# A state-space scan and a memory attention in one kernel: V projection moved beside the scan, Q/K projection interleaved with a key-by-query attention

## The chip, the cores and the metric

One core of one Trainium2 chip. The time is device microseconds of that core, the median of several executions; lower is better. Engine names: PE is the matmul engine and PEld its weight loads, DVE the vector engine, ACT the scalar engine, POOL the GpSimd engine, SP the engine that here only issues DMA. "L336" in a profile line is line 336 of the kernel that was profiled.

## The reference, cut to what matters

The output is two unrelated results side by side: part A is a complex diagonal state-space scan over 2048 steps with 1024 states; part B is an attention over 64 segments of 32 tokens, each of which also sees 8 memory rows, where the memory of a segment is the output of the segment before it.

```python
def _A_ref(x, Lambda_re, Lambda_im, B_re, B_im, C_re, C_im, log_dt, Dskip):   # x: 1 x 2048 x 1024
    # ... Lam_bar, B_bar from the parameters ...
    Bu = jnp.einsum('bld,pd->blp', x + 0j, B_bar)
    for t in range(L):
        h = Lam_bar[None, :] * h + Bu[:, t, :]
        hs.append(h)
    y = 2.0 * jnp.einsum('blp,dp->bld', hseq, Cmat).real + x * Dskip[None, None, :]

def _B_ref(x, mem0, Wq, Wk, Wv, Wo, seg_len):      # 32 heads of 128, M = 8, seg_len = 32
    for s in range(n_seg):
        xs = x[:, s * seg_len:(s + 1) * seg_len, :].copy()
        h = jnp.concatenate([mem, xs], axis=1)
        q = jnp.einsum('btd,dhe->bhte', h, Wq)     # k and v likewise
        scores = jnp.einsum('bhqe,bhke->bhqk', q, k) * scale
        scores = jnp.where(mask[None, None], scores, -1000000000.0)
        p = _softmax(scores, axis=-1)
        o = jnp.einsum('bhqk,bhke->bhqe', p, v)
        o = jnp.einsum('bhte,hed->btd', o, Wo)
        mem = o[:, :M, :].copy()
        outs.append(o[:, M:, :])
return jnp.concatenate([a, b], axis=-1)
```

Both kernels avoid the 64 sequential steps in the same way. They guess every segment's memory from the mean of its rows, compute all segments at once with the guess, compare the memory that comes out with the guess, and repeat in a slower way only if the two differ by more than a tolerance (2^-8).

One caution for all that follows. With these inputs the attention half of the reference has a standard deviation of 2.0e-5 and the scan half of 2.5e-3 (computed from the reference). A comparison over the whole output therefore hardly sees an error in the attention half.

## The kernel before

It runs four stages one after the other: part A (scan and its output matmuls); K, V and mean projections of all tokens; Q projection with the guess and the projections of the guessed memory; attention with the output projection. K, V and Q go to DRAM and come back. A unit is 4 segments and 16 heads: scores have queries on partitions, so the probabilities must be transposed by DVE before the product with V, and the memory rows of V are gathered from DRAM in 16 small pieces per unit.

```python
        def load(u):
            g, hh = units[u]; h0 = hh * HH
            d = {}
            e1 = nc.sync
            e2 = nc.scalar
            d["kT"] = ld.tile([128, HH, J, L], BF16, name="s2_kT")
            e2.dma_start(d["kT"][:], scr["kTa"][g, :, h0:h0 + HH, :, :])
# ... cut ...
            d["v"] = ld.tile([128, HH * E], BF16, name="s2_v")
            e2.dma_start(d["v"][:], scr["v"][g * 128:(g + 1) * 128, h0 * E:(h0 + HH) * E])
            vx = vmx[u % NBUF]
            for j in range(J):
                for b in range(4):
                    r0 = (g * J + j) * M
                    src = scr["vm"][r0:r0 + M, h0 * E:(h0 + HH) * E].rearrange("k (a b e) -> k a b e", b=4, e=E)[:, :, b, :]
                    dst = vx[32 * j + 8 * b:32 * j + 8 * b + 8, :, :].rearrange("k (a b) e -> k a b e", b=4)[:, :, b, :]
                    (nc.sync if (j * 4 + b) % 2 == 0 else nc.scalar).dma_start(dst, src)
            d["vx"] = vx
            S.activation(d["kT"][:, :, :, 0:M], km_u[:], ACT.Copy)
```

Softmax in `front`, and the transposes (`PTx`, `PTm`), then the products in `back`:

```python
            mx = sm_.tile([128, nh], FP32, name=f"s2_mx{tag}")
            V.tensor_reduce(mx[:], Sx[:], AX.X, ALU.max)
            Gp.tensor_tensor(Sx[:], Sx[:], mx[:].unsqueeze(2).to_broadcast([128, nh, L]), ALU.subtract)
            S.activation(Sx[:], Sx[:], ACT.Exp)
            sm = sm_.tile([128, nh], FP32, name=f"s2_sum{tag}")
            V.tensor_reduce(sm[:], Sx[:], AX.X, ALU.add)
            V.reciprocal(sm[:], sm[:])
            Px = sm_.tile([128, nh, SEG], BF16, name=f"s2_Px{tag}")
            Pm = sm_.tile([128, nh, M], BF16, name=f"s2_Pm{tag}")
            Gp.tensor_tensor(Px[:], Sx[:, :, M:L], sm[:].unsqueeze(2).to_broadcast([128, nh, SEG]), ALU.mult)
            Gp.tensor_tensor(Pm[:], Sx[:, :, 0:M], sm[:].unsqueeze(2).to_broadcast([128, nh, M]), ALU.mult)
            return Px, Pm
# ... cut ...
                Px, Pm = softmax(pl, HH, cst["maskx"], "x")
                ptx = PTx[u % 2]; ptm = PTm[u % 2]
                for j in range(J):
                    q = slice(32 * j, 32 * j + 32)
                    V.transpose(ptx[q, j, :, :].rearrange("p h k -> p (h k)"), Px[q, :, :].rearrange("p h k -> p (h k)"))
                    V.transpose(ptm[q, j, :, :].rearrange("p a k -> p (a k)"), Pm[q, :, :].rearrange("p h m -> p (h m)"))
# ... cut ...
        def back(u):
            g, hh = units[u]; h0 = hh * HH
            d = st[u]; v_u = d["v"]; vx = d["vx"]
            if do_x:
                ptx = PTx[u % 2]; ptm = PTm[u % 2]
                oT = op_.tile([128, HH, 128], BF16, name="s2_oT")
                for a in range(HH // 4):
                    pO = psO.tile([128, 4, 128], FP32, name="s2_pO")
                    for b in range(4):
                        h = 4 * a + b
                        PE.matmul(pO[:, b, :], v_u[:, h * E:(h + 1) * E], ptx[:, :, h, :], start=True, stop=False)
                        PE.matmul(pO[:, b, :], vx[:, h, :], ptm[:, :, a, :], start=False, stop=True)
                    S.activation(oT[:, 4 * a:4 * a + 4, :], pO[:], ACT.Copy)
```

## Time and profile before

| | before |
|---|---|
| time, median of 3 runs | 1677.34 us (1676.97 to 1678.32) |
| span of the profiled run, mean granted PE clock | 1670.9 us, 0.950 |
| PE busy, idle | 1458.8 us, 212.1 us |
| DMA | 233.72 MB in 224776 packets |

The first part of the profile page: busy time of each engine, its share of the span, and how many instructions.

```profile
span 1670.9 us, 33806 instructions
PE 1458.8 (87%) x14297; PEld 764.0 (46%) x14297; DVE 828.3 (50%) x1869; ACT 425.4 (25%) x793; POOL 148.9 (9%) x240
```

The windows view cuts the span into stretches; the columns are the stretch, its length, the busy time and the number of instructions of each engine, the granted PE clock (1.00 is full), the DMA share and GB/s.

```profile
core 0: us, PE busy (x) PEld busy (x) DVE busy (x) ACT busy (x) POOL busy (x), PEclk, DMA share, GB/s
0.00:348.00 348.00, 287.70 (x1673) 144.68 (x1674) 320.27 (x670) 129.65 (x228) 20.45 (x39) 0.94 0.22 67
348.00:860.00 512.00, 510.53 (x3246) 240.40 (x3246) 103.97 (x165) 84.84 (x145) 8.48 (x4) 1.00 0.45 151
860.00:1160.00 300.00, 252.89 (x2067) 134.36 (x2066) 89.79 (x177) 60.00 (x110) 3.36 (x7) 0.94 0.68 203
1160.00:1671.00 511.00, 407.72 (x7312) 244.58 (x7311) 314.24 (x857) 150.93 (x310) 116.57 (x191) 0.92 0.46 141
```

Length minus PE busy is the time in which PE stands still: 60 us in part A, where DVE is the busy one, 1.5 us in the projections, 47 us in the third stage, and 103 us in the attention. In the attention stage the clock is 0.92 as well, so the matmuls themselves take longer.

The waits view (what an engine waited for; total us, how often, longest) names for the attention stage, on PE and on ACT:

```profile
ACT s_kT L516 <- DMA s_vmx_10121<-b_vm_s: 64.8, 13, 7.3
ACT s_kT L516 <- DMA s_vmx_10122<-b_vm_s: 54.1, 15, 11.2
PE s_pO L586 <- DVE s_PTx_10123 L567: 36.4, 13, 5.1
PE s_pO L586 <- DVE s_PTx_10124 L567: 28.8, 11, 3.1
```

Read alone, the lines of PE say that the DVE transposes cost 65 us, and the lines of ACT that the memory gathers (`s_vmx`) make only ACT wait, which is 30% busy here.

### The profile page before, as it was taken

Reading aid. Unit: us, or ns where it says so; the run is one execution under the profiler, and the core shown is the slowest. Engines: PE = TensorE matmul, PEld = TensorE weight load, DVE = VectorE, ACT = ScalarE, POOL = GpSimd, SP = SyncE. Lnnn points to the kernel's source line nnn. Section 1 sums busy time; section 2 is a strip of 40 time slices with the busy share of each in tenths; the row PEclk is TensorE's granted clock in tenths of the full one; section 3 lists DMA queues with packets and bytes.
Section 4 is the critical chain, followed back from the end, with each engine's and each line's share of the span. In section 5 each row is a group of like instructions: output and inputs, shape, how many; then the busy total and the mean of one; then the engine's idle time right before and its main releaser. Section 6 shows DMA issues by size and latency. Waiting matters only on the chain.

```text
span 1670.9 us, 33806 instructions
## 1 busy us (share of the span) xinstructions
PE 1458.8 (87%) x14297; PEld 764.0 (46%) x14297; DVE 828.3 (50%) x1869; ACT 425.4 (25%) x793; POOL 148.9 (9%) x240
## 2 busy tenths in 40 slices
PE   4789989889999999999999888992888777887787
PEld 2444434444444444444445444441545444454454
DVE  8999999631221121121223322223656666566564
ACT  7742322111111111111121122221223232323322
POOL 1100000020000000000000000001222222222220
PEclk9899999899999999999999999996899999999999
DMA  3430000296415424432363689865444545545432
GB/s 114 128 97 15 28 16 20 82 309 218 138 53 190 139 76 166 139 115 102 121 207 108 195 257 273 252 177 186 130 146 145 157 136 162 159 136 163 136 109 96
DMA packets 224776, 233.72 MB, mean 140 GB/s; under 512 B 61536, under 2 KB 197472, under 8 KB 224616
## 3 DMA queue, kind: packets, MB, share of 16 engines
q1 hardware_dynamic: 154272, 129.08, 25.3%
q10 hardware_dynamic: 68024, 95.04, 17.4%
q0 software_dynamic: 2320, 7.35, 1.3%
q8 instruction: 114, 1.87, 0.5%
q14 instruction: 46, 0.38, 0.1%
HBM read 150.99 MB, written 80.45 MB: 139 GB/s over the span
## 4 chain that ended last, share of the span: by engine, by line
PE 57%; DVE 25%; DMA 8%; POOL 4%; ACT 3%; issue 2%; SPq 1%; ACTq 0%; POOLq 0%; DVEq 0%
PE p_p L320 13%; PE p_p L336 13%; PE p_p L723 11%; DVE a_wr L178 2%; DVE a_wi L179 2%; DVE s_PTx_10123 L567 2%; PE s_pO L587 2%; PE s_pO L586 2%; POOL s_Sxx L534 2%; DVE s_PTx_10124 L567 1%; DMA p_wm<-in_B_Wk_dram 1%; POOL s_Pxx L541 1%; DVE s_Sxx L530 1%; DVE s_mxx L533 1%; DVE s_sumx L537 1%
## 5 line engine op out<-in xcount | busy, mean ns | idle before, releaser
L336 PE MATMUL p_p<-p_w,g_shared 128*128 128x512 bf16 x1024 | 224.6, 379 | 0.0
L723 PE MATMUL p_p<-g_shared,p_w 128*128 128x512 bf16 x896 | 198.9, 381 | 0.3 <-DVE p_stq L261 0.2
L320 PE MATMUL p_p<-g_shared,p_w 128*128 128x512 bf16 x896 | 194.5, 379 | 0.0
L612 PEld LDWEIGHTS <-s_oT 128*128 128x128 bf16 x1024 | 100.1, 103 | 128.8 <-issue 28.9
L336 PEld LDWEIGHTS <-g_shared 128*128 128x128 bf16 x1024 | 98.4, 98 | 118.4 <-issue 2.6
L261 DVE CAST p_stk<-p_p 128x512 bf16<-128x512 f32 x64 | 44.3, 692 | 191.7 <-PE p_p L320 185.8
L723 PEld LDWEIGHTS <-p_w 128*128 128x128 bf16 x896 | 87.2, 98 | 106.4 <-issue 5.4
L320 PEld LDWEIGHTS <-p_w 128*128 128x128 bf16 x896 | 87.1, 98 | 104.1
L261 DVE CAST p_st<-p_p 128x512 bf16<-128x512 f32 x64 | 44.3, 692 | 180.7 <-PE p_p L336 180.7
L261 DVE CAST p_stq<-p_p 128x512 bf16<-128x512 f32 x64 | 44.2, 691 | 168.0 <-PE p_p L723 167.2
L259 ACT ACTIVATE p_st<-p_p 128x512 bf16<-128x512 f32 x64 | 38.2, 597 | 200.7 <-PE p_p L336 200.7
L586 PEld LDWEIGHTS <-s_v 128*128 128x128 bf16 x512 | 53.4, 106 | 77.6 <-issue 38.9
L166 PEld LDWEIGHTS <-g_shared 128*128 128x128 bf16 x512 | 51.7, 102 | 70.9 <-issue 22.6
L259 ACT ACTIVATE p_stk<-p_p 128x512 bf16<-128x512 f32 x64 | 38.2, 597 | 179.1 <-PE p_p L320 167.6
L166 PE MATMUL a_ur<-a_xT,g_shared 128*128 128x512 bf16 x256 | 70.2, 412 | 9.1 <-DVE a_ta L174 9.1
L534 POOL TENSOR_TENSOR s_Sxx<-s_Sxx,s_mxx 128x640 f32<-128x640 f32 x32 | 40.4, 1262 | 405.8 <-DMA s_km<-b_kmT_s 252.1
L586 PE MATMUL s_pO<-s_PTx_10123,s_v 128*128 128x128 bf16 x256 | 39.8, 238 | 41.6 <-DVE s_PTx_10123 L567 36.4
L588 ACT ACTIVATE s_oT<-s_pO 128x512 bf16<-128x512 f32 x128 | 69.8, 592 | 24.1 <-PE s_pO L587 23.9
L214 PE MATMUL a_py<-a_CT_137,a_h 128*128 128x512 bf16 x256 | 67.6, 389 | 9.1 <-DVE a_h L195 9.1
L259 ACT ACTIVATE p_stq<-p_p 128x512 bf16<-128x512 f32 x64 | 37.8, 596 | 139.5 <-PE p_p L723 114.4
L534 POOL TENSOR_TENSOR s_Sxm<-s_Sxm,s_mxm 128x160 f32<-128x160 f32 x34 | 15.4, 454 | 608.9 <-DVE s_mxm L533 608.9
L586 PE MATMUL s_pO<-s_PTx_10124,s_v 128*128 128x128 bf16 x256 | 38.7, 236 | 33.0 <-DVE s_PTx_10124 L567 28.8
(573 smaller groups left out, 2320.3 us busy)
## 6 DMA issues: line engine op xcount, KB each, us to landing
s_kT<-b_kTa_s ACTq DMA_DIRECT2D x34, 640.0 KB
b_kTa_s<-p_stk ACTq DMA_DIRECT2D x8, 2560.0 KB
s_v<-b_v_s ACTq DMA_DIRECT2D x34, 512.0 KB
b_v_s<-p_st SPq DMA_DIRECT2D x16, 1024.0 KB
b_qT_s<-p_stq SPq DMA_DIRECT2D x16, 1024.0 KB
s_qT<-b_qT_s SPq DMA_DIRECT2D x32, 512.0 KB
p_w<-in_B_Wq_dram SPq DMA_DIRECT2D x15, 1024.0 KB
p_w<-in_B_Wv_dram SPq DMA_DIRECT2D x8, 1024.0 KB
```

Of the source, the lines that this page charges most:

```text
L166: PE.matmul(u[:], BT[i][:, kc, pc * 128:(pc + 1) * 128], xT[:, kc, :], start=(kc == 0), stop=(kc == KC - 1))
L214: PE.matmul(py[:], hs[pc][:, 0, tt * 128:(tt + 1) * 128], CT[0][:, pc, half * 512:(half + 1) * 512], start=(pc == 0), stop=False)
L259: self.nc.scalar.activation(out, in_, ACT.Copy)
L261: self.nc.vector.tensor_copy(out, in_)
L320: PE.matmul(p[:], w[1][:, c, h4 * 128:(h4 + 1) * 128], xT[:, c, tb * 512:(tb + 1) * 512], start=(c == 0), stop=(c == KC - 1))
L336: PE.matmul(p[:], xT[:, c, tt * 128:(tt + 1) * 128], w[2][:, c, :], start=(c == 0), stop=(c == KC - 1))
L534: Gp.tensor_tensor(Sx[:], Sx[:], mx[:].unsqueeze(2).to_broadcast([128, nh, L]), ALU.subtract)
L567: V.transpose(ptx[q, j, :, :].rearrange("p h k -> p (h k)"), Px[q, :, :].rearrange("p h k -> p (h k)"))
L586: PE.matmul(pO[:, b, :], v_u[:, h * E:(h + 1) * E], ptx[:, :, h, :], start=True, stop=False)
L588: S.activation(oT[:, 4 * a:4 * a + 4, :], pO[:], ACT.Copy)
L612: PE.matmul(pY[:], st[2 * gi + h // HH]["oT"][:, h % HH, :], Wo_sb[:, h, half * 512:(half + 1) * 512], start=(h == 0), stop=(h == H - 1))
L723: PE.matmul(p[:], wq[:, c, h4 * 128:(h4 + 1) * 128], xT[:, c, tb * 512:(tb + 1) * 512], start=(c == 0), stop=(c == KC - 1))
```

## The change

The intent was to keep PE busy throughout by putting PE work beside the stages that other engines pace, and to drop work and DMA of the attention:

- The V projection of one head block (128 matmuls of 512 columns) runs beside four units of the scan. Part A's states go to DRAM, and its output matmuls become a stage of their own beside the guess.
- Q and K are projected per pair of heads and stay in SBUF. The projection of the next pair is interleaved with the attention of this one.
- Attention is key-by-query: scores come out with keys on partitions, so nothing is transposed. The softmax sum comes from a matmul with a matrix of ones, its reciprocal from exp(-ln(x)) on ACT, and no maximum is subtracted. The mask is a product on POOL.
- A unit is two groups of three segments for two heads; each group has 96 tokens and 3 memory rows. Where the 8 guessed memory rows of a segment are the same row, one key with weight 8 in the mask stands for them.
- If the check fails, a loop over the 64 segments in order computes part B anew.

The file changed nearly everywhere. The core of the diff, with cuts marked:

```diff
@@ load of a unit, softmax, transposes (before) @@
-            vx = vmx[u % NBUF]
-            for j in range(J):
-                for b in range(4):
-                    r0 = (g * J + j) * M
-                    src = scr["vm"][r0:r0 + M, h0 * E:(h0 + HH) * E].rearrange("k (a b e) -> k a b e", b=4, e=E)[:, :, b, :]
-                    dst = vx[32 * j + 8 * b:32 * j + 8 * b + 8, :, :].rearrange("k (a b) e -> k a b e", b=4)[:, :, b, :]
-                    (nc.sync if (j * 4 + b) % 2 == 0 else nc.scalar).dma_start(dst, src)
# ... cut ...
-                ptx = PTx[u % 2]; ptm = PTm[u % 2]
-                for j in range(J):
-                    q = slice(32 * j, 32 * j + 32)
-                    V.transpose(ptx[q, j, :, :].rearrange("p h k -> p (h k)"), Px[q, :, :].rearrange("p h k -> p (h k)"))
-                    V.transpose(ptm[q, j, :, :].rearrange("p a k -> p (a k)"), Pm[q, :, :].rearrange("p h m -> p (h m)"))
@@ attention unit (after) @@
+    def att_front(self, hp, u):
+        k = self.k; PE = k.PE
+        qt, kt = self.qk[hp % 2]
+        s = k.ps("S", (128, 2, 2, GW))
+        for gg in range(2):
+            g0 = (2 * u + gg) * GW
+            for hh in range(2):
+                PE.matmul(s[:, gg, hh, :], kt[:, hh, g0:g0 + 128], qt[:, hh, g0:g0 + GW], start=True, stop=True)
+        e = self.p3a.tile([GW, 2, 2, GW], BF16, name="b_e", bufs=3)
+        i = hp * NU + u
+        k.S.activation(e[:], s[0:GW], ACT.Exp, scale=float(E) ** -0.5, accum_out=self.accE[0:GW, i:i + 1])
+        m = self.p3a.tile([GW, 2, 2, GW], BF16, name="b_m", bufs=4)
+        mask = k.maskA if u == 0 else k.maskB
+        k.G.tensor_tensor(m[:], e[:], mask[0:GW, :, :].unsqueeze(2).to_broadcast([GW, 2, 2, GW]), ALU.mult)
+        return m
+
+    def att_back(self, hp, u, m):
+        k = self.k; PE, V = k.PE, k.V
+        vt = self.vtile[hp]
+        sm = k.ps("R")
+        W4 = 4 * GW
+        mf = m[:].rearrange("p a b q -> p (a b q)")
+        PE.matmul(sm[:, 0:W4], k.ones[0:GW, :], mf, start=True, stop=True)
# ... cut ...
+        k.S.activation(ln[:], sm[:, 0:W4], ACT.Ln)
+        k.S.activation(r[:].rearrange("p a b q -> p (a b q)"), ln[:], ACT.Exp, scale=-1.0, accum_out=self.accR[:, i:i + 1])
+        o = k.ps("O", (128, 2, 2, GW))
+        for gg in range(2):
+            for hh in range(2):
+                PE.matmul(o[:, gg, hh, :], vt[:, 2 * u + gg, hh * 128:(hh + 1) * 128], m[:, gg, hh, :], start=True, stop=True)
+        ot = self.ot[hp]
+        V.tensor_tensor(ot[:, :, 2 * u * GX:(2 * u + 2) * GX].rearrange("p h (g n) -> p g h n", n=GX),
+                        o[:, :, :, 0:GX], r[:, :, :, 0:GX], ALU.mult)
# ... cut ...
@@ projection of a head pair (after); one yield per group of matmuls @@
+            for q in range(4):
+                for i in range(2):
+                    t = self.qk[hp % 2][i]
+                    for hh in range(2):
+                        p = k.ps("P")
+                        for c in range(KC):
+                            PE.matmul(p[:, 0:480], w[i][:, c, hh * 128:(hh + 1) * 128], self.xe[:, c, 480 * q:480 * q + 480],
+                                      start=(c == 0), stop=(c == KC - 1))
+                        g0 = (1 + 5 * q) * GW
+                        k.copy("v", t[:, hh, g0:g0 + 5 * GW].rearrange("p (g n) -> p g n", n=GW)[:, :, 0:GX],
+                               p[:, 0:480].rearrange("p (g n) -> p g n", n=GX))
+                        yield
@@ stage 1: scan unit, then four groups of V matmuls @@
+            for pc in range(PC):
+                v = b.v_x(pc, wv)
+                nxt = None
+                for tb in range(NB):
+                    if pc == 0 and tb + 1 < NB:
+                        a.load_x(tb + 1)
+                    a.stage1(pc, tb)
# ... cut ...
+                    for _ in range(4):
+                        next(v, None)
@@ stage 3: projection steps spread over the attention units @@
+            pr, at = b.proj(), b.attention()
+            b.v_mem(0)
+            for _ in range(14):
+                next(pr)
+            done = 14
+            k.SP.dma_start(wo0[:], b.Wo[:, :, 0:512])
+            for n, (hp, u) in enumerate(at):
+                if u == 4 and hp % 2 == 0 and hp + 2 < HP:
+                    b.v_mem(hp // 2 + 1)
+                want = min(18 * HP, 14 + (n + 1) * 18 // 11)
+                while done < want:
+                    next(pr)
+                    done += 1
```

## The prediction

> **What bounds the kernel now.** TensorE. The page gives PE 1458.8 of 1670.9 us busy (87%), DVE 50%, ACT 25%; PE holds 57% of the chain that ended last. The windows view shows four stages:
> - 0-348 us, part A (scan): DVE is busy 40.00 of 40 us from 80 to 160; the timeline shows one scan unit (512 steps, 128 states) every 8.5 us of DVE; PE needs 7.5.
> - 348-860, K, V, first Q projections: PE 100% busy, clock 1.00.
> - 860-1160, rest of Q, memory guess and projections: the chain holds four loads or stores of 10-12 us.
> - 1160-1656, attention and output projection: PE busy 401 of 496 us, clock mostly 0.93, waiting for DVE transposes and 544 small gathers of memory V.
>
> In the timeline 16 matmuls of 512 columns take 3.46 us (216 ns each); 128-column ones start 56 ns apart. That is columns/2.4 GHz + 2.5 ns, as the Trainium skill (TensorE: Matmul & The Clock Gate, "Back-to-back issue gap") has it. I estimate with 216, 202 (480 columns), 86 (201), 56 (128) and 44 ns (99).
>
> **PE work of the change (estimates).** The old kernel, costed so, holds about 1385 us; some 290 us is waiting or half clock. The new one:
> - Stage 1, scan with V projection: 1536 x 216 ns = 332, 512 transposes 29, guess columns 19: 380 us.
> - Stage 2, A's output, guess: 576 x 216 = 124.
> - Stage 3, Q/K projection with attention: 2048 x 202 + 512 x 86 = 459, memory V 14, attention 176 units x (8 x 44 + 167) = 92: 565.
> - Stage 4, output projection, check: 235.
>
> Sum 1304: only 80 us less work. Gone are Q/K trips through DRAM, DVE transposes, memory gathers and thousands of tiny matmuls. Added: a 396-column ones-matmul per unit, h's round trip through DRAM, second loads of Wv and Wo. Most of the gain must be waits.
>
> **Other engines (estimates).**
> - Stage 1: DVE 32 x 8.5 + 8 tables x 3.9 + 15 = 318 us; ACT 205. PE-bound, tightly.
> - Stage 3: DVE 330 (256 evictions x 0.66, 176 x 0.7, small copies), ACT 320-350 (three passes of 396 elements, 0.53 us each from the 160- and 640-element ones), POOL 150.
>
> **Waits left (estimates).** Start 12; first scan block 20; scan coupling 20; stage-2 start, 2 MB h load, 15; stage-3 fill and last units without projection 22; stage-4 start, up to 8 MB of loads, 13; end 8; unlisted 20. Sum 130.
>
> **Predicted 1440 us, 8 in 10 between 1390 and 1530.** Faster by over 2%: 0.95; within 2%: 0.02; slower: 0.03.
>
> **In the profile, if right.** Stage ends near 430, 570, 1160, 1430. PE over 90% busy, clock 0.97 or better. In stage 3 Q/K matmuls lead the chain and no other engine is over 65%. DMA falls from 234 to about 155 MB. Idle PE sits at stage boundaries.
>
> **What would make it wrong.**
> - The sequential fallback firing: milliseconds. Emulating the roundings, I find the check at 0.74-0.89 of its tolerance, so it should stay off.
> - Stage 1: V evictions queue on ACT behind copies that wait for the scan; three PSUM buffers cover 5 us of PE. DVE pacing would add 40-60 us.
> - Stage 3: sums have one PSUM buffer and a chain through POOL, PE, ACT twice, DVE. If a unit's round trip passes its 3.2 us of PE work, the stage grows to it.
> - Ln and Exp not sharing one activation table: a load took 1.28 us; 352 would add hundreds.

## More of the kernel before

The word "DMA" in the lines of ACT misleads. The timeline of one unit (start, length, engine, line, operation, and in brackets the wait that the profile names) shows what ACT did meanwhile:

```profile
1311.58 3.46 ACTq L514 DMA_DIRECT2D s_vmx_10122<-b_vm_s  x8
1315.09 0.63 ACT L516 ACTIVATE s_kT<-s_km 128x512 bf16<-128x512 bf16 x1 [3.18 <-DMA s_vmx_10122<-b_vm_s]
```

ACT issues 8 of the unit's 16 gathers itself, ahead of its copy, and issuing is not counted as busy. In all 28 of these waits the copy starts within 0.1 us of the last of the 8 issues, so it waits for ACT's own issuing (63 us of the 119 are the issues themselves, the rest stands between them) and not for the last data to land.

## The result, and the profile after

| | before | after |
|---|---|---|
| time, median of 4 runs each of the same rounds | 1677.15 us | 1419.89 us |
| lowest and highest | 1675.85, 1678.32 | 1414.53, 1422.01 |
| span of the profiled run, mean granted clock | 1670.9 us, 0.950 | 1420.3 us, 0.975 |
| PE busy, idle | 1458.8, 212.1 us | 1335.1, 85.2 us |
| DMA | 233.72 MB | 163.20 MB |

The ratio is 0.8465 (95% interval 0.8446 to 0.8484). Ratios here are from the runs of the same rounds; they differ from the ratio of the medians that are quoted by 0.0015 at most. The kernel before took between 1671.6 and 1677.2 us on the chips that were used, so from here on differences between two kernels are differences of their ratios times 1677 us; these ratios have intervals of about 0.002, or 3 us, each way, so such a difference is uncertain by some 5 us.

The page after:

```profile
span 1420.3 us, 20776 instructions
PE 1335.1 (94%) x8087; PEld 697.2 (49%) x8162; DVE 665.4 (47%) x1495; ACT 488.7 (34%) x1203; POOL 208.0 (15%) x283
```

The windows view by stage (columns as before): scan with V; part A's output with the guess; a hole; Q/K projection with attention; its last units; output projection.

```profile
0.00:435.00 435.00, 395.45 (x2240) 196.49 (x2281) 325.88 (x653) 193.25 (x297) 19.22 (x87) 0.98 0.37 118
435.00:571.00 136.00, 128.41 (x572) 58.91 (x585) 24.37 (x39) 1.44 (x3) 33.95 (x16) 0.96 0.51 183
571.00:592.00 21.00, 0.27 (x1) 0.14 (x1) 0.93 (x13) 0.00 (x0) 0.00 (x0) 0.56 1.04 337
592.00:1157.00 565.00, 565.00 (x4125) 327.97 (x4124) 291.72 (x736) 267.93 (x833) 147.01 (x170) 1.00 0.35 100
1157.00:1176.00 19.00, 9.60 (x86) 5.92 (x86) 8.70 (x29) 13.76 (x48) 7.78 (x11) 0.68 0.97 312
1176.00:1420.00 244.00, 236.36 (x1067) 107.81 (x1087) 13.84 (x27) 12.37 (x24) 0.00 (x0) 0.98 0.22 71
```

From 592 to 1157 us PE is busy in every one of the 565 us, at full clock, while DVE, ACT and POOL work at 52%, 47% and 26% beside it. What is left of idle PE is 40 us in the first stage, 21 in the hole and 25 in the three other windows. Of the span's fall of 250.6 us, 123.7 is PE's busy time and 126.9 its idle time.

The waits of PE after; the hole is the first line:

```profile
PE psP L451 <- DMA b_wv<-in_B_Wv_dram: 21.2, 1, 21.2
PE psP L210 <- DMA a_stg<-in_A_x_dram: 18.2, 6, 9.8
PE psP L615 <- DMA b_ol<-b_os_96: 5.4, 1, 5.4
```

The transposes and the gathers have no counterpart. The groups view (busy us, mean ns of one; then the idle time ahead) shows what took their place in the attention, four passes over a unit and two reads of accumulators:

```profile
L534 ACT ACTIVATE b_e<-psS 99x396 bf16<-99x396 f32 x176 | 88.5, 503 | 374.5 <-PE psS L531 370.8 <-PE psO L555 2.4 <-POOL b_m L537 1.2
L534 ACT ACTIVATION_READ_ACCUMULATOR b_e<-psS 99x1 f32 x176 | 34.6, 197 | 0.0
L550 ACT ACTIVATE b_ln<-psR 128x396 f32<-128x396 f32 x176 | 87.1, 495 | 0.0
L551 ACT ACTIVATE b_r<-b_ln 128x396 f32<-128x396 f32 x176 | 94.2, 535 | 5.4
L551 ACT ACTIVATION_READ_ACCUMULATOR b_r<-b_ln 128x1 f32 x176 | 33.3, 189 | 0.0
L537 POOL TENSOR_TENSOR b_m<-b_e,maskB 99x396 bf16<-99x396 bf16 x160 | 139.8, 873 | 348.8 <-ACT b_e L534 348.8
```

Ln and Exp alternate 352 times here, and the whole trace holds three table loads of 1283 ns, none of them in this stage. That agrees with the Trainium skill (ScalarE: Activation LUTs, "Table sets: the hidden batching unit"), which lists one set that has both exp and ln.

The 21.2 us hole, on SP's queue and on PE. The columns of the timeline are start, length, engine, line, operation, and in brackets the wait ahead of it.

```profile
570.61 0.39 SPq L851 DMA_DIRECT2D t_5172<-in_B_Wo_dram  x1
571.39 8.08 SPq L302 DMA_DIRECT2D out_dram<-a_ot  x1
579.53 0.42 SPq L477 DMA_DIRECT2D b_wq<-in_B_Wq_dram  x1
...
582.91 2.96 SPq L375 DMA_DIRECT2D b_wv<-in_B_Wv_dram  x1
```

```profile
564.74 5.78 PE L298 MATMUL psO<-t_111,a_hl 128*128 128x512 bf16 x25
591.73 3.57 PE L451 MATMUL psP<-b_wv,b_xe 128*73 128x512 bf16 x8 [21.21 <-DMA b_wv<-in_B_Wv_dram]
```

At 570.61 us SP issues the 4 MB load of half of Wo, which is not read until 1176 us. The store behind it takes 8.08 us to issue, the small loads that stage 3 starts with are issued 9 to 12 us after the big one, and `b_wv`, which the first matmul reads, is there at 591.7. In the program the 4 MB load stands last of these; the scheduler put it first.

### The profile page after: what moved, and what is told of

The parts are those of the page before. It is cut to its first block, busy times and chain, and to the rows that moved or that the text cites. A ratio compares the mean times of both kernels' runs of the same rounds, so it can differ in the third digit from the quotient of the medians.

```text
span 1420.3 us, 20776 instructions
## 1 busy us (share of the span) xinstructions
PE 1335.1 (94%) x8087; PEld 697.2 (49%) x8162; DVE 665.4 (47%) x1495; ACT 488.7 (34%) x1203; POOL 208.0 (15%) x283
## 2 busy tenths in 40 slices
DMA packets 159742, 163.20 MB, mean 115 GB/s; under 512 B 9152, under 2 KB 132656, under 8 KB 159128
## 5 line engine op out<-in xcount | busy, mean ns | idle before, releaser
L388 PE MATMUL psP<-b_wv,b_xe 128*128 128x512 bf16 x1006 | 228.2, 381 | 1.1
L507 PE MATMUL psP<-b_xe,b_wk 128*128 128x480 bf16 x1024 | 225.8, 365 | 0.0
L507 PE MATMUL psP<-b_xe,b_wq 128*128 128x480 bf16 x1024 | 223.4, 365 | 0.0
L537 POOL TENSOR_TENSOR b_m<-b_e,maskB 99x396 bf16<-99x396 bf16 x160 | 139.8, 873 | 348.8 <-ACT b_e L534 348.8
L557 DVE TENSOR_TENSOR b_ot<-psO,b_r 128x384 bf16<-128x384 f32 x176 | 98.2, 558 | 192.0 <-ACT b_r L551 178.8
L388 PEld LDWEIGHTS <-b_xe 128*128 128x128 bf16 x1024 | 99.9, 98 | 118.3 <-issue 2.4
L507 PEld LDWEIGHTS <-b_wq 128*128 128x128 bf16 x1024 | 95.7, 97 | 93.7
L507 PEld LDWEIGHTS <-b_wk 128*128 128x128 bf16 x1024 | 95.4, 97 | 92.6
L298 PE MATMUL psO<-t_111,a_hl 128*128 128x512 bf16 x500 | 114.0, 386 | 4.4 <-DMA a_hl<-a_hs_76 3.7
L615 PE MATMUL psP<-t_5172,b_ol 128*128 128x512 bf16 x438 | 101.5, 386 | 5.8 <-DMA b_ol<-b_os_96 5.4
L615 PE MATMUL psP<-wo_12598,b_ol 128*128 128x512 bf16 x438 | 98.9, 379 | 0.5
```

The costliest lines, as they stand in the source:

```text
L298: PE.matmul(py[:], hl[:, pc, i, tt * 128:(tt + 1) * 128], self.CT[:, i, pc, hs], start=(pc == 0 and i == 0), stop=(pc == PC - 1 and i == 1))
L388: k.PE.matmul(p[:], self.xe[:, c, t * 128:(t + 1) * 128], w[:, c, :], start=(c == 0), stop=(c == KC - 1))
L507: PE.matmul(p[:, 0:480], w[i][:, c, hh * 128:(hh + 1) * 128], self.xe[:, c, 480 * q:480 * q + 480], start=(c == 0), stop=(c == KC - 1))
L537: k.G.tensor_tensor(m[:], e[:], mask[0:GW, :, :].unsqueeze(2).to_broadcast([GW, 2, 2, GW]), ALU.mult)
L557: V.tensor_tensor(ot[:, :, 2 * u * GX:(2 * u + 2) * GX].rearrange("p h (g n) -> p g h n", n=GX), o[:, :, :, 0:GX], r[:, :, :, 0:GX], ALU.mult)
L615: PE.matmul(p[:], lhs, self.wo[half][:, h, :], start=(h == 0), stop=(h == H - 1))
```

## The experiments

Twelve kernels were run, all correct by the comparison above. The theories to tell apart:

- T1: the two pairings (V beside the scan, attention beside the projection) each hide work worth 100 us or more, and stage 3 is bound by PE alone.
- T2 (rival): the gain comes from the smaller work and DMA of the new attention; pairing matters little.
- T3 (rival): stage 3 is bound by the chain of one unit through ACT, POOL and PE, or by ACT.
- About the gain against the kernel before: how much of it was gathers and transposes.

| run | base | median us | ratio to before | against its base |
|---|---|---|---|---|
| v_after_scan | after | 1563.09 | 0.9320 | +143 us |
| att_in_turn | after | 1553.03 | 0.9262 | +134 us |
| exp_twice | after | 1418.58 | 0.8461 | -1 us |
| sum_one_head | after | 8107.63 | 4.8339 | fallback ran |
| sum_one_head2 | after | 1401.36 | 0.8378 | -15 us |
| wo_late | after | 1407.09 | 0.8411 | -9 us |
| wv_late | after | 1425.42 | 0.8521 | +9 us |
| both_late | after | 1416.11 | 0.8463 | 0 us |
| b_few_gathers | before | 1599.64 | 0.9555 | -75 us |
| b_few_both | before | 1563.96 | 0.9346 | -110 us |
| stage3_best | after | 1398.54 | 0.8346 | -20 us |
| all_best | after | 1381.71 | 0.8257 | -35 us |

### v_after_scan: the V projection after the scan

```diff
             for pc in range(PC):
-                v = b.v_x(pc, wv)
# ... cut ...
                 for tb in range(NB):
# ... cut ...
                     a.stage1(pc, tb)
# ... cut: the loads of Wv go from here to the new loop ...
-                    for _ in range(4):
-                        next(v, None)
# ... cut ...
+        with pool("p1v", "right") as p1v:
+            b.vst = p1v
+            wv = b.load_wv(0, p1v)
+            for pc in range(PC):
+                nxt = b.load_wv(pc + 1, p1v) if pc + 1 < PC else None
+                for _ in b.v_x(pc, wv):
+                    pass
+                b.og(pc, wv)
```

> V projection taken out of the scan loop and run after it. Theory (V fills TensorE while VectorE runs the scan): the scan alone is paced by VectorE, 32 units x 8.5 us plus 8 tables x 3.9 us plus the start, so it ends near 335-345 us; V then needs 8 x (27.6 + 1.9) = 236 us and a short fill, so this part ends near 585 us in place of 435 and the whole takes about 1570 us (1550-1590). Rival (the pairing gained little, the two slow each other down): under 1480 us.

Measured: 1563.09 us, 143 us slower. The windows of the scan alone, then of V alone:

```profile
100.00:300.00 200.00, 118.74 (x525) 53.19 (x536) 199.86 (x403) 63.61 (x88) 0.00 (x0) 0.80 0.18 57
340.00:575.00 235.00, 232.78 (x1075) 104.34 (x1095) 2.33 (x8) 80.64 (x135) 0.00 (x0) 1.00 0.31 99
```

The same stretch of the kernel after:

```profile
100.00:300.00 200.00, 197.12 (x975) 91.24 (x993) 165.17 (x318) 84.47 (x138) 0.00 (x0) 1.00 0.34 108
```

Alone, the scan keeps DVE busy in 199.86 of 200 us and PE in 118.74, at a clock of 0.80; the V matmuls then take another 238 us (333 to 571) at full clock. Side by side, PE is busy 197 of 200 us. Not all of the 143 us is lost pairing: this run asks for its first Wv only when the scan has ended (327 us), and PE waits 23.6 us for it. A version that loads it earlier might lose some 120 us (an estimate, 143 less 23.6; not run). The Trainium skill (Perfetto Trace Analysis, "Optimization Strategy") suggests interleaving stretches whose most-contended engine differs, and this run puts 120 to 143 us on it. The clock agrees with the skill's description of a gate that follows how busy PE has been recently (TensorE: Matmul & The Clock Gate, "What's actually happening"): 0.80 here and 1.00 in the dense stretch.

### att_in_turn: projection and attention in turn, not interleaved

The 11 attention units of a head pair, then the 18 projection steps of the next pair, in an order that the scheduler may not change.

```diff
-            for _ in range(14):
+            for _ in range(18):
                 next(pr)
# ... cut ...
-            for n, (hp, u) in enumerate(at):
+            for n in range(HP * NU + 2):
+                hp, u = in_turn(at)
# ... cut ...
-                want = min(18 * HP, 14 + (n + 1) * 18 // 11)
-                while done < want:
-                    next(pr)
-                    done += 1
+                if u == NU - 1 and done < 18 * HP:
+                    for _ in range(18):
+                        in_turn(pr)
+                        done += 1
# ... cut: in_turn() orders what it issues behind the last PE instruction ...
```

> TensorE's order forced: all 18 projection steps of a head pair, then its 11 attention units, no mixing. Theory (the projections fill the time in which a unit goes through ScalarE, GpSimd and VectorE): the units then run at the pace of the last, projection-less units of the new kernel, about 1.39 us each, so 176 x 1.39 = 245 us of units plus 473 us of projections in place of 583 us: about +135 us, near 1555 us (1530-1590), and the granted clock falls. Rival (the units' own chain already paces the stage at 3.2 us each): the projections come on top in full, over 1800 us. Other rival (mixing is worth nothing): within 20 us of 1420.

Measured: 1553.03 us, 134 us slower. The waits of PE get one new leading line, and the windows view of most of stage 3 shows the clock:

```profile
PE psR L546 <- POOL b_m L537: 54.3, 134, 1.1
```

```profile
640.00:1300.00 660.00, 606.84 (x3891) 339.88 (x3890) 291.10 (x699) 231.26 (x818) 143.43 (x168) 0.90 0.28 81
```

Alone, a unit takes 1.39 us from one ones-matmul to the next, for some 0.5 us of PE work; PE waits 0.4 us at a time for POOL's mask product (54.3 us over 134 waits), and the clock falls to 0.90 over the stage. Interleaved, the same matmuls run at 1.00 with no wait. Of the 130 us by which the span is longer (1549.9 against 1420.3), 78 are PE busy time with the same matmuls (1413.5 against 1335.1), the lower clock, and 51 are idle. T2 falls: undone one at a time, each pairing costs about half of the whole gain of 257 us.

### exp_twice: one ACT pass more per unit

```diff
         k.S.activation(e[:], s[0:GW], ACT.Exp, scale=float(E) ** -0.5, accum_out=...)
+        k.S.activation(e[:], s[0:GW], ACT.Exp, scale=float(E) ** -0.5)
```

> Each unit's exponential is computed twice on ScalarE, 0.5 us more per unit, 88 us of ScalarE in all; result unchanged. Theory (ScalarE has slack in stage 3, about 50% busy): within 6 us of 1420, the last 9 units being the only place where it shows. Rival (ScalarE or a chain through it paces the stage): +40 to +88 us.

Measured: 1418.58 us, no difference (1 us). Stage 3 with it:

```profile
592.00:1160.00 568.00, 564.85 (x4157) 328.37 (x4155) 291.44 (x746) 321.11 (x1024) 150.15 (x175) 1.00 0.35 100
```

ACT is busy 321 us against 268 in 565 us of the kernel after, and every unit's chain is longer by 0.5 us, yet PE keeps its 565 us. T3 falls.

### sum_one_head and sum_one_head2: fewer columns in the ones-matmul

The sums are taken for one of the four (group, head) pairs only and used for all four, 99 columns instead of 396. The attention values are wrong on purpose.

```diff
-        PE.matmul(sm[:, 0:W4], k.ones[0:GW, :], mf, start=True, stop=True)
+        PE.matmul(sm[:, 0:GW], k.ones[0:GW, :], mf[:, 0:GW], start=True, stop=True)
-        k.S.activation(ln[:], sm[:, 0:W4], ACT.Ln)
+        k.S.activation(ln[:].rearrange("p (a q) -> p a q", a=4), sm[:, 0:GW].unsqueeze(1).to_broadcast([128, 4, GW]), ACT.Ln)
```

> The ones-matmul of each unit takes 99 columns of one head in place of all 396, and ScalarE reads that sum four times, so only TensorE has less to do: 297 columns x 0.417 ns = 124 ns less per unit. (Wrong in general; here the scores are nearly 0 and the sums nearly equal, so it may still pass, except that the first unit's masks differ by group.) Theory (stage 3 is paced by TensorE): -22 us, near 1398 us. Rival (paced by the unit's chain through the other engines): within 5 us of 1420.

Measured: 8107.63 us. The expectation missed. It named the cause as a reservation, that in unit 0 the two groups have different masks, but did not count on it: their sums differ, so the memory must have come out wrong for the check to see it, and the fallback ran: 6700 us in the trace, 64 iterations of 105 us. The fallback computes part B anew, so what such a run returns is not the wrong values. The part ahead of the loop can still be read: stage 3, from its first matmul to the first one of the output projection, took 563.5 us against 584.2.

sum_one_head2 leaves unit 0 alone (`WS = W4 if u == 0 else GW`).

> As sum_one_head, but each head pair's first unit keeps its full sum, since its two groups have different masks; that should keep the check quiet and the sequential fallback off. 160 units x 124 ns less TensorE work. Theory (stage 3 paced by TensorE): -20 us, near 1400 us. Rival (the unit's chain): within 5 us of 1420. If the fallback fires again: over 8000 us.

Measured: 1401.36 us, 15 us faster by the ratios; stage 3 took 564.8 us by the trace, 19.3 less than after. The columns taken away are 160 units x 297, which at 2.4 per ns are 19.8 us (512 columns take 216 ns and 128 take 56 in these traces, so 384 columns more take 160 ns). The 15 us by the ratios and the 20 that were expected agree within the 5 us above. So stage 3 follows PE's columns one for one. With exp_twice this shows that PE sets its length; DVE and POOL were not slowed by any run, but PE leaves them no wait to answer for (busy 565 of 565 us).

### wo_late, wv_late, both_late: the order of loads

wo_late moves the 4 MB load behind stage 3's first loads and forbids the scheduler to move it. wv_late keeps the 1 MB loads of Wv in stage 1 in the program's order too; in the kernel after the scheduler issues the first two of them at 1.7 us, after two tiles of x and ahead of the rest, and PE then waits 9.8 us for x. both_late does both.

```diff
@@ wo_late @@
-            k.SP.dma_start(wo0[:], b.Wo[:, :, 0:512])
             for n, (hp, u) in enumerate(at):
+                if n == 1:
+                    tc.keep_in_program_order(k.SP.dma_start(wo0[:], b.Wo[:, :, 0:512]))
@@ wv_late, in load_wv @@
-        self.k.SP.dma_start(w[:], self.Wf[2][:, :, hb * 512:(hb + 1) * 512])
+        i = self.k.SP.dma_start(w[:], self.Wf[2][:, :, hb * 512:(hb + 1) * 512])
+        if pool is self.vst:
+            self.k.tc.keep_in_program_order(i)
```

> The 4 MB load of half of Wo, which the scheduler put at the head of the queue at the start of stage 3, is issued after the first attention units instead. Theory (the 21.2 us hole in TensorE at 570-592 us is the queue's order: 4 MB of data not needed for 600 us go ahead of 2 MB of weights needed at once): the hole shrinks to about 9-10 us, -8 to -14 us, near 1409 us. Rival (the hole is the wait for SBUF that stage 2 still holds, or plain load time): within 4 us of 1420.

> In stage 1 the Wv loads stay in program order on the queue; in the new kernel two of them, 2 MB, go ahead of the third and fourth tiles of x, for which TensorE waits 9.8 us at 6.6-16.5 us. Theory (same cause at the start): the first scan unit starts about 9 us sooner and the whole gains 5 to 10 us. Rival (the first scan block is paced by the loads of both x in any order): within 3 us.

> Both orders of the queue mended. Theory: the two gains add, -13 to -24 us, near 1401 us. If they don't add, one of the two explanations is wrong.

Measured: wo_late 1407.09 us, 9 us faster; the hole shrank from 21.2 to the 9.8 us of this line of its waits, with the small loads issued first:

```profile
PE psP L451 <- DMA b_wv<-in_B_Wv_dram: 9.8, 1, 9.8
```

wv_late missed: 1425.42 us, 9 us slower, where 5 to 10 us of gain were expected. The scan's first matmul did come earlier (15.3 us against 23.1). But now the second Wv load, kept in its place, stood in the same queue as stores that wait for the scan. SP's queue (a line may hold several issues and spans them all), then PE:

```profile
36.10 8.84 SPq L276 DMA_DIRECT2D a_hs<-a_h  x2
44.99 0.43 SPq L375 DMA_DIRECT2D b_wv<-in_B_Wv_dram  x1
...
46.27 9.32 SPq L207 DMA_DIRECT2D a_stg<-in_A_x_dram  x4
```

```profile
53.34 1.89 PE L210 MATMUL psP<-ident,a_stg 128*128 128x128 bf16 x16 [8.31 <-DMA a_stg<-in_A_x_dram]
```

The end of the second scan unit on DVE:

```profile
44.17 0.42 DVE L275 TENSOR_TENSOR a_h<-a_n,a_n 128x512 bf16<-128x512 bf16 x1
```

The first line of SP holds two stores of scan states: the first was issued at 36.1, the second at 44.6, the moment DVE had finished its data (44.17 + 0.42). For those 8 us nothing else left the queue; the pinned load and the next tiles of x came behind it, and PE stood still for 8.31 us waiting for x. That uses up the early start: the mean matmuls of the first head block begin at 101.9 us, where they began at 103.7 in the kernel after and at 98.3 in wo_late, whose stage 1 is the same program as in the kernel after. Most of the loss lies later. From there to the same matmuls of the eighth block it takes 334 us here and 335 in both_late, against 328 in the kernel after and in wo_late; the difference sits in three blocks between 236 and 390 us, where PE waits 7.1 us for B, the scan's input matrix, in place of 3.6, and falls to half clock twice for 3.4 us. In each of the three, the pinned 1 MB load of Wv enters SP's queue 1.2 us ahead of the loads of B (310.31 and 311.54 us in one of them), where the scheduler had put it some 22 us ahead (290.37 and 311.96): once more a load that nobody needs yet ahead of one that is needed at once, this time by the pin. (This is read from the traces; no run pins single loads.) all_best, which pins only the first two, takes 327 us. both_late: 1416.11 us, the sum of the two single changes (-9 and +9) within the spread.

### b_few_gathers, b_few_both: the kernel before without gathers and transposes

Of the 16 memory gathers per unit 4 are kept. Each now brings its rows for all 16 heads and not for 4 (32 KB in place of 8), so the bytes stay (233.68 MB against 233.72), but three heads of four find them in the wrong rows. In b_few_both one of four rounds of transposes is kept as well. The matmuls stay: 14297 PE instructions in all three. b_few_both also sets the flag of the check to 0, so that its loop stays off.

```diff
             for j in range(J):
-                for b in range(4):
+                for b in range(1):
                     r0 = (g * J + j) * M
-                    src = scr["vm"][r0:r0 + M, h0 * E:(h0 + HH) * E].rearrange("k (a b e) -> k a b e", b=4, e=E)[:, :, b, :]
-                    dst = vx[32 * j + 8 * b:32 * j + 8 * b + 8, :, :].rearrange("k (a b) e -> k a b e", b=4)[:, :, b, :]
+                    src = scr["vm"][r0:r0 + M, h0 * E:(h0 + HH) * E].rearrange("k (a e) -> k a e", e=E)
+                    dst = vx[32 * j:32 * j + 8, :, :]
@@ b_few_both also, for the token and memory parts alike @@
-                for j in range(J):
+                for j in range(1):
                     q = slice(32 * j, 32 * j + 32)
                     V.transpose(ptx[q, j, :, :]..., Px[q, :, :]...)
```

> The kernel BEFORE, with 4 gathers of memory V per attention unit in place of 16 (each brings 8 rows of all 16 heads; the mixing of memory V is then wrong for three heads of four, which changes the result little). Theory (part of the old kernel's idle TensorE time after 1160 us, 103 us, was waiting for these gathers: 36 us of weight-load waits and 119 us of ScalarE's kT copies name them): -10 to -40 us, near 1650. Rival (they were off the path): within 5 us of the kernel before.

> The kernel BEFORE with the 4 gathers and only the first of each unit's four rounds of VectorE transposes (the result is wrong on purpose for three segments of four; the flag of the check is forced to 0). It takes 4.3 us of VectorE per unit, 137 us in all, out of the chain from scores to P times V; TensorE's work is unchanged. Theory (the old attention stage was held by the chain through VectorE, not by TensorE's work): -40 to -90 us, near 1615. Rival (TensorE's own work held it and the gain of the change came from removed matmuls): under 15 us more than b_few_gathers gives.

Measured: 1599.64 us, 75 us faster, where 10 to 40 were expected; and 1563.96 us, another 35 faster, 110 in all where 40 to 90 were expected. Both expectations missed on the low side: the gathers cost more than the waits seemed to say. The attention stage of each:

```profile
1160.00:1598.00 438.00, 374.75 (x7184) 234.20 (x7184) 308.75 (x856) 145.03 (x306) 114.91 (x190) 0.98 0.52 163
```

```profile
1160.00:1560.00 400.00, 372.31 (x7184) 232.40 (x7183) 174.57 (x465) 145.41 (x302) 114.13 (x188) 0.99 0.57 177
```

The waits of PE for the first of them, where all transposes are still there:

```profile
PE s_pO L586 <- ACT s_oT L588: 32.1, 26, 1.7
PE s_pO L586 <- DVE s_PTx L567: 3.5, 1, 3.5
```

In the kernel before PE waited 65 us for the transposes; with a quarter of the number of gathers it waits 3.5 us for the same transposes, and 32 us for ACT's copies instead. So the 65 us were for the most part the gathers', passed on: ACT's copy of the memory keys, which the scores need, had waited 119 us on them, and the transposes only stood last in the chain. The 4 gathers that are left are all issued by SP, so ACT issues none of its 8 any more. That their place ahead of ACT's copy was the cost, and not their number, is what the timeline of the kernel before suggests (ACT's 28 waits are its own issuing); 16 gathers all issued by SP were not run. From 511 us to 400 the stage lost 111 us; 35 of them are PE busy time (407.7 to 372.3 in the window, 1458.8 to 1423.7 over the whole runs with the same 14297 matmuls), that is the clock, which rose from 0.92 to 0.99.

### stage3_best and all_best: does this lead to a faster version?

stage3_best takes wo_late, and loads stage 3's first weights during stage 2 into buffers that are opened earlier; the projection leads by 8 steps in place of 14. all_best adds three things: the stores of the first scan block go out on POOL's queue, so that loads of x don't stand behind them; the first two Wv loads are kept in order and the second is asked for later; and the second half of Wo comes in four parts, behind the loads that the output projection starts with. In both the attention values are computed as in the kernel after.

```diff
@@ stage3_best @@
+        b.p3w = p3w.enter_context(pool("p3w", "left"))
             for i, _ in enumerate(s2):
+                if i == 16:
+                    b.wv0 = b.load_wv(0, b.p3w)
+                    b.load_wqk(0)
# ... cut: wo_late, lead 14 -> 8 ...
@@ all_best adds @@
-        k.SP.dma_start(self.hs[tb][:, pc, :, :], h[:])
+        (k.G if pc == 0 else k.SP).dma_start(self.hs[tb][:, pc, :, :], h[:])
# ... cut: the same for the first V stores; two pinned Wv loads ...
-            k.SP.dma_start(wo1[:], b.Wo[:, :, 512:D])
             ol = b.load_o(0)
+            for q in range(4):
+                tc.keep_in_program_order(k.SP.dma_start(wo1[:, 8 * q:8 * q + 8, :], b.Wo[:, 8 * q:8 * q + 8, 512:D]))
```

> The new kernel with the first Wv, Wq and Wk blocks of stage 3 in SBUF of their own and loaded during stage 2, half of Wo loaded later, and the projections leading attention by 8 steps in place of 14, so that fewer units at the end run without projection. Theory (the 21.2 us hole is load order and load time only): the hole falls to 4 us or less, -17 us, and the shorter tail gives another 3 to 4: near 1399 us (1394 to 1405). Rival (stage 3 cannot start before stage 2 has drained and freed SBUF): no better than wo_late, near 1407.

> stage3_best with three more changes of the queues' order. Start: the first Wv load stays behind the first x tiles and B, the second goes behind the last x tile, and the h and V stores of the first block, which must wait for compute, go out on GpSimd's queue, so that no x load stands behind them (that is what I take to have eaten the gain of wv_late: its first scan matmul came 7 us sooner, then an x tile came 8.3 us late behind an h store on the same queue). Stage 4: the O loads go ahead of the second half of Wo, which is split in four. Theory: -5 to -10 us at the start, kept this time, and -3 to -6 us at stage 4: near 1387 us (1380 to 1393). Rival for the start (the first block is paced by the two-deep staging of x, whatever the order): first block ends as before, near 104 us, and the whole is near 1394.

Measured: stage3_best 1398.54 us, 20 us faster than after. The hole at stage 3's start is gone, but by its timeline PE now waits 10.4 us at the start of the output projection, where it was 5.4. all_best 1381.71 us (1378.84 to 1383.17), 35 us faster than after, and the fastest kernel. Its stages:

```profile
0.00:424.00 424.00, 394.32 (x2234) 196.64 (x2276) 324.64 (x650) 191.42 (x295) 25.04 (x95) 0.98 0.37 121
424.00:560.00 136.00, 127.90 (x579) 58.74 (x590) 24.50 (x40) 3.00 (x4) 33.90 (x16) 0.97 0.63 217
560.00:1133.00 573.00, 570.33 (x4209) 331.94 (x4207) 299.68 (x772) 281.33 (x877) 154.49 (x180) 1.00 0.37 107
1133.00:1380.00 247.00, 235.58 (x1072) 107.95 (x1091) 15.62 (x33) 13.58 (x29) 0.00 (x0) 0.98 0.26 86
```

```profile
PE psP L210 <- DMA a_stg<-in_A_x_dram: 10.2, 6, 2.9
PE psP L616 <- DMA wo<-in_B_Wo_dram: 1.4, 2, 0.8
```

The hole is gone, the wait for x is 10.2 us where it was 18.2, and in place of 5.4 us for `b_ol` the output projection waits 1.4 us for parts of Wo. How the 15 us over stage3_best divide among the three additions was not run. By the two traces part A's output matmuls begin 9.6 us earlier (435.7 against 445.3 us; 439.7 to 445.3 in the traces whose stage 1 is unchanged), and the 10.4 us wait at the output projection is gone. PE is busy 1328 of 1379 us.

## Why the prediction was right, and which terms were off

It said 1440 us (1390 to 1530), and 1419.9 was measured. By steps:

- "TensorE" bounds the kernel, and "most of the gain must be waits". Both held. PE work was put at 1385 us before and 1304 after, a fall of 80; PE busy fell by 123.7, of which at least 35 is clock and not work, as the experiments on the kernel before show, so some 89 at most is work. Idle PE fell by 126.9 us. Waiting and half clock, which the prediction counts together, are thus at least 162 of the 250.6 us.
- Stage ends were put "near 430, 570, 1160, 1430". They were 435, 571, 1170 (last attention matmul) and 1420. The PE work of stage 3, put at 565 us, is 574.6 us of busy PE (565.00 and 9.60 in its two windows).
- "PE over 90% busy, clock 0.97 or better" and "no other engine is over 65%" in stage 3: 94%, 0.975, and 52% at most. "From 234 to about 155 MB": 163 MB. "Q/K matmuls lead the chain" could not be checked, because the chain of waits of the kernel after came out as a single piece; in the groups view these matmuls are the second and third largest groups.
- The four dangers did not come true in this kernel: the fallback stayed off (sum_one_head shows what it costs when it fires, 6700 us); stage 1 was not paced by DVE (V and scan together leave PE busy 197 of 200 us); the single PSUM buffer of the sums did not pace stage 3, which takes another ACT pass without loss; Ln and Exp shared a table set. The figures given for the check, 0.74 to 0.89 of its tolerance, were not tested by any run.
- Terms mis-sized. That the total came within 20 us is partly luck, because two errors offset each other. PE work was put too low: 1304 us, where PE was busy 1335.1 (by stages 395, 128, 575 and 236, where 380, 124, 565 and 235 were put). The waits were put too high: 130 us, where PE was idle 85.2. "Scan coupling 20" and "unlisted 20" were too high: PE is idle 40 us in the whole first stage, where start, first block and coupling were put at 52, and nothing unlisted was found. So were the starts of stages 2 and 4, put at 15 and 13: PE is idle 8 us in the whole second stage and waits 5.4 for `b_ol`. "Stage-3 fill and last units 22" came out at about 25, but not as thought: the hole is 21.2, and the last units leave only some 4 us idle (19.0 less 9.6 busy, less the 5.4 for `b_ol`). The estimate had not seen that a 4 MB load would be issued ahead of the loads needed at once. ACT in stage 3 was put at 320 to 350 us and is 268 in the 565 us window.

Where the gain came from, as far as the runs show. Gathers and transposes of the old attention, with the slow clock that came with them, are worth 110 us (b_few_both, which issues a quarter of the gathers and of the large and small transposes). The pairings are worth 120 to 143 and 134 us in the new kernel. These are not parts of one sum. Moving V beside the scan brought next to nothing over the kernel before, if one adds up durations (this was not run as a version of the kernel before): that one hid part A's output matmuls under the scan, and its part A with all V matmuls (348 us, and 1024 x 216 ns = 221 us) takes 569 us, while the new kernel's first two stages end at 571, the guess included. It is the right use of the scan's idle PE, and costs 120 to 143 us if undone, but it replaced another use. From b_few_both (span 1560.5) to after is another 140 us. 89 of them are PE busy (1423.7 to 1335.1), and by the windows the other 52 are idle time: 26 in the first two stages (65 us idle) against stage 1 (40), 15 in the stage of guess and memory projections (43) against stage 2 and the hole (28), 11 in the attention and what follows (28 against 17). That last split is bookkeeping over stages that differ, not an experiment, and which of the removed loads and stores made those 52 us stays open.

## What to carry to other kernels

Find which engine paces each stage, and pair a stage that PE paces with one that it doesn't; before counting that as gain, ask what the old kernel already hid there. A wait is named after whatever came last: look who made that one late before costing it, or take it away and measure. Look also at what the waiting engine issues meanwhile: here 119 us of "waits for DMA" on ACT were its own issuing of DMAs, with the pauses between the issues. At the boundary of stages, look at the order in which loads and stores stand in the issuing queue: a big load that nobody needs yet, or a store whose data aren't ready, makes everything behind it late. all_best gained 35 us by the order, time and queue of loads and stores, with buffers opened earlier and a shorter lead. Pinning an order can cost as well: wv_late lost 9 us.

## What the Trainium skill lacked or had wrong

- TensorE: Matmul & The Clock Gate, "Back-to-back issue gap", gives N/2.4 + 2.5 ns for an isolated matmul and, as a sustained figure, about 131 ns at 512 columns and 81 ns at 128. In these traces streams of 512-column matmuls run 216 ns apart (16 in 3.46 us) and 128-column ones 56 ns apart. The formula held in dense streams with weight loads between; the sustained figures did not.
- ScalarE: Activation LUTs mentions an accumulator output but no cost. Here each activation with one is followed by a separate instruction that reads the accumulator, 197 and 189 ns on average, 352 times and 68 us in all in stage 3.
- DMA: Bandwidth & Descriptors, "Issuing engines are not separate DMA queues", says that several issuing engines save only the time to issue, usually small beside the DMA itself. In the kernel before, the 8 gathers that ACT issues in each unit delay its copy by 119 us in all. In wv_late a store whose data were not ready held SP's queue for some 8 us (36.4 to 44.6) and PE waited 8.31 us for a load behind it. In all_best, where such stores went to another issuing engine among other changes, PE waits 10.2 us for x in place of 18.2.
- No page says, as far as I found, that the order of loads in one queue can cost PE time at the boundary of stages: a 4 MB load issued ahead of small ones made a hole of 21.2 us, and moving it left 9.8.
